# Two small weight loads issued by ScalarE in place of SyncE, at the head of a long-convolution and MLP kernel

## The chip, the cores and the metric

The kernel runs on one core of one Trainium2 chip. The metric is the device time of one execution in microseconds (us). The engines are named as in the profile: PE is TensorE (PEld its weight loads), ACT is ScalarE, DVE is VectorE, POOL is GpSimd and SP is SyncE. SP issues nearly all memory transfers; ACT can issue them as well, and in this kernel issues two. The data move on the core's 16 DMA engines. Rows marked SPq and ACTq show the time in which an engine issues a transfer, not the time in which the data move.

## The reference

Two layers stand in turn, each twice. Layer A is a gated long convolution: `k` is filtered with a four-tap causal filter per channel (`shift_k`), multiplied by `v`, convolved over the whole sequence with `ssm_k`, given a skip term `ssm_D`, and multiplied by the normalised input. Layer B is an MLP with a GELU.

```python
def _A_ref(q, k, v, shift_k, ssm_k, ssm_D):
    k_pad = jnp.pad(k, ((0, 0), (ks - 1, 0), (0, 0)))
    for t in range(ks):
        k_shift = k_shift + k_pad[:, t:t + S, :] * shift_k[:, ks - 1 - t]
    kv = k_shift * v
    ...
    y = irfft(rfft(kv) * rfft(ssm_k))[:S]
    y = y + kv * ssm_D
    return q * y
x = A_q
x = x + _A_ref(_layernorm(x), A_k, A_v, A_shift_k, A_ssm_k, A_ssm_D)
x = x + _B_ref(_layernorm(x), B_w1, B_b1, B_w2, B_b2)
x = x + _A_ref(...)
x = x + _B_ref(...)
```

Here S is 2048, D is 512, the MLP is 1376 wide, and all inputs are bf16. `shift_k` is 512 x 4: four kilobytes.

## The kernel before, in words

Since `kv` depends on `k` and `v` alone, the convolution is computed once and used by both A layers. The program has two parts. In the first, an order written out by hand (the string `ORDER`, L18 to L20) says which named piece stands next and on which engine: `lk1.S` is the piece `lk1` on SP, `kT1e.A` the evacuation of `kT1` on ACT, `P3` a PE piece that takes the third PSUM buffer. Each engine runs its pieces in that order. The second part (from L676) is the MLP, with PE bound by its matmuls.

What matters here is the head of the first part. Before the `ORDER` begins, the prologue issues two transfers from ACT, `Ft` (a table, L185) and four copies of `ssm_D` (L186), and lets POOL clear `kT` (L192) and spread `ssm_D` into `Dz` (L194). Then the pieces:

- `lSK` loads the weights of the last 128 channels as one row of 512 numbers (1 KB, the view `SKr`). `bSK` (L407) is a matmul that copies this row to all partitions, the first thing that PE does; ACT evacuates it (`bSKe`). POOL's filter of those channels uses it (`tap`, L435).
- `lsT` loads the weights of all 512 channels with a channel in each partition, as 128 x 4 runs of four numbers (8 bytes each). POOL casts it (`sF`, L361), and DVE builds twelve diagonal matrices from it (`dg`, L417), the weights of the filter on PE.
- `lk0` to `lk3` load `k` in four quarters of 512 KB; `lh1` and `lh113` load three rows before each partition's `k` (`kh`). `lx0` loads the first quarter of the input (512 KB, from `in_A_q_dram`), `lv0` and `lv1` load `v` (1 MB each), `lK00` to `lK11` load `ssm_k`.
- `kT1`, `kT3`, `kT0`, `kT2` (L423) transpose three channel groups of the four quarters of `k` on PE, in that order, each after its load. ACT evacuates the first three, DVE the last. `kv10`, `kv21`, `kv11`, `kv00` (L506) are the filter on PE, and DVE multiplies their results by `v` (L512).
- `s00` takes the layernorm sums of the first quarter of the input on ACT (L469 to L472). On ACT it stands behind the three evacuations and ahead of `U1S0e`, the evacuation of the convolution's first stage, for which PE waits.

Every transfer that SP or ACT issues has one of eight completion counters, named DMAHW0 to DMAHW7, which are handed out in turn in the order of the program text: `Ft` has 0, `ssm_D` 1, `lSK` 2, `lk1` 3, `lsT` 4, and so on. The ninth transfer has counter 0 again, and its issuer first waits until the transfer that had it before has landed.

Of the kernel before, what the change touches and what calls it, by code (L numbers as in the profile page):

```python
# [104 lines left out]
def kernel(ctx: ExitStack, tc: tile.TileContext, A_q, A_k, A_v, A_shift_k, A_ssm_k, A_ssm_D,  # L105
                 B_x, B_w1, B_b1, B_w2, B_b2, out):
    nc = tc.nc
    P = 128
    _, S, D = A_q.shape
    F = B_w1.shape[1]  # L110
    KS = A_shift_k.shape[1]
    NT = S // P
    CT = D // P
# [25 lines left out]
    def at(off, dims, p0=0, n=P):  # L139

        return apf(arena, p0 * ROW + off // 2, [[ROW, n]] + dims)
# [17 lines left out]
    CK = CT - 1  # L159
# [15 lines left out]
    B1 = const.tile([P, FT], F32, name="B1")  # L175
# [7 lines left out]
    nc.gpsimd.memset(IDt[:], 1.0)  # L183
    nc.gpsimd.affine_select(IDt[:], IDt[:], [[-1, P]], ALU.is_equal, 0.0, base=0, channel_multiplier=1)
    nc.scalar.dma_start(Ft[:], F_h.ap().bitcast(BF16))  # L185
    nc.scalar.dma_start(apf(arena, 40 * K, [[32 * ROW, 4], [1, D]]), apf(A_ssm_D, 0, [[0, 4], [1, D]]))  # L186
    nc.gpsimd.memset(b1T[:], 0.0)
    h = KS - 1
# [86 lines left out]
    with tc.tile_pool(name="ps", bufs=1, space=bass.MemoryType.PSUM) as ps:  # L275
# [3 lines left out]
        def load(name, dst, src, nbytes, deps=(), eng="S", rank=0):  # L279
            return plan.add(name, {eng: 400}, deps, lambda it: nc.sync.dma_start(dst, src), dma=("copy", nbytes), rank=rank)  # L280
# [5 lines left out]
        def mm_evac(name, ns, deps, mms, dims, dst, bf=False, take=(), free_mm=(), edeps=(), rank=0, src=None):  # L286
            src = src or (lambda v: v)
            n = int(np.prod(dims))
            cost = {"A": 85 + 0.82 * n, "D": 50 + (0.53 if bf else 1.06) * n}
            pe = plan.add(name, {"P": ns}, deps, lambda it: mms(view(pf[it["slot"]["ps"]], dims, BF16 if bf else None)),  # L290
                          take=["ps"] + list(take), free=free_mm, rank=rank)
            ev = plan.add(name + "e", cost, [pe] + list(edeps),
                          lambda it: evac(it["eng"], dst(), src(view(pf[pe["slot"]["ps"]], dims, BF16 if bf else None))),
                          free=[(pe, "ps")], rank=rank)
            return pe, ev
# [47 lines left out]
        kd4 = k_d.rearrange(TOK, p=P)  # L343
# [3 lines left out]
        for c in range(NK):  # L347
            n = 64 // NK
            lK.append([])
            for par in range(2):  # L350
# [3 lines left out]
                                      dma=("small", 2 ** 21 // (2 * NK))))  # L354
        lk = [load(f"lk{q}", kn[:, 4 * q:4 * q + 4, :], kd4[:, 4 * q:4 * q + 4, :], 2 ** 19) for q in range(4)]
        lv = [load(f"lv{o}", uv[:, 8 * o:8 * o + 8, :], vd[:, 8 * o:8 * o + 8, :], 2 ** 20) for o in range(2)]
        lS = [load("lsT", sT[:], A_shift_k.rearrange("(ct p) k -> p ct k", p=P), 2 ** 17),
              load("lSK", SKr, apf(A_shift_k, CK * P * KS, [[P * KS, 1], [1, P * KS]]), 2 ** 13)]
        lS += [load(f"lh{p0}", kh[p0:p0 + n, :, :], apf(k_d, (16 * p0 - h) * D + CK * P, [[16 * D, n], [D, h], [1, P]]), 2 ** 17)
               for p0, n in ((1, 112), (113, 15))]  # L360
        sf = plan.add("sF", {"G": 100}, lS[:1], lambda it: nc.gpsimd.tensor_copy(sF[:], sT[:]))  # L361
        lW = load("lW", Wt[:], W_h.ap().bitcast(BF16), 2 ** 20)
        lX = load("lX", Wx[:], X_h.ap().bitcast(BF16), 2 ** 20)
        lH = load("lH", GPt[:], GP_h.ap().bitcast(BF16), 2 ** 16)
# [36 lines left out]
        for j in range(4):  # L401
            r = slice(8 * j, 8 * j + 8)
            KX.append([load(f"s{w}{j}", KSW[a::2, r, :], ZK[1 - a::2, r, :], 1.15 * 2 ** 19, KW[4 * j:4 * j + 4] + (KWp if j == 3 else []))
                       for w, a in (("a", 0), ("b", 1))])


        _, bSK = mm_evac("bSK", 250, lS[1:2], lambda o: nc.tensor.matmul(o, one[:], SKr, start=True, stop=True), [P * KS],  # L407
                         lambda: SK[:])
# [40 lines left out]
        kgm = plan.add("kgm", {"D": 1150, "G": 4200}, kg[-1:] + lv, gmul)  # L449
# [8 lines left out]
        lx0 = load("lx0", lna0, xd[:, 0:GT, :], 2 ** 19)  # L458
        lx1 = load("lx1", x1, xd[:, GT:2 * GT, :], 2 ** 19)
# [33 lines left out]
        s10, _ = first(1, x1, lx1)  # L493
# [24 lines left out]
        lM = load("lM", Mt[:], M_h.ap().bitcast(BF16), 2 ** 21, kvp)  # L518
# [5 lines left out]
        lx = load("lx", x_t[:], q_d.rearrange(TOK, p=P), 2 ** 21, USp)  # L524
# [284 lines left out]
```

## Time and profile before

| | us |
|---|---|
| median of three runs | 253.29 (253.15 to 253.44) |
| profiled execution, its own time | 253.65 |
| its span, first to last instruction | 251.9 |
| PE busy | 236.9 (94%) |
| ACT busy | 146.5 (58%) |
| DVE busy | 169.7 (67%) |
| first transfer issued (SP and ACT) | 0.80 |
| first filter matmul on PE (L506) | 13.22 |

PE is nearly always busy, but the first 20 us are not its own: there it waits for loads and for ACT and DVE. A gain or a loss at the head moves everything behind it, as long as no wait behind it takes it up. In a row of the time line, the first number is the start, the second the length, and the bracket at the end says how long the engine was idle before it and what ended that.

### The profile page before, as it was taken

The page shows a single profiled execution, that of the slowest core. Times are in us where ns is not written, and L with a number is a line of the kernel's source. Part 1 is how long each engine was busy: PE and PEld are TensorE (multiplying, and loading weights), DVE is VectorE, ACT ScalarE, POOL GpSimd, SP SyncE. Part 2 cuts the span into 40 slices and gives each one's busy share as a digit, 9 for nine tenths or more (in the row PEclk, how much of TensorE's full clock was granted, in tenths as well). Part 3 has the DMA queues.
Part 4 walks back from the last instruction along what each step waited for, and adds up shares of the span by engine and source line. Part 5 has one row for each costly group of instructions (what it writes and reads, how often), then busy time and mean ns, then how long its engine had stood idle before and what let it go on. Part 6 is the DMA issues. An engine that isn't in the chain of part 4 may idle for free.

```text
span 251.9 us, 5135 instructions
## 1 busy us (share of the span) xinstructions
PE 236.9 (94%) x2104; PEld 146.1 (58%) x2104; DVE 169.7 (67%) x319; ACT 146.5 (58%) x212; POOL 54.6 (22%) x52
## 2 busy tenths in 40 slices
PE   2688999999999999999999999999999999999995
PEld 1588767899998738844444444444444444444443
DVE  0335889989999794987889899886866862022022
ACT  3598899999999798903803803803703712712810
POOL 3199999510000011011111101110110110000000
DMA  5999994698929993022040403107006006001001
GB/s 130 367 349 183 239 428 191 209 390 300 232 44 181 175 318 113 0 48 39 1 83 0 86 0 61 22 0 86 1 28 139 3 25 143 0 23 64 0 21 62
DMA packets 53040, 30.15 MB, mean 120 GB/s; under 512 B 46642, under 2 KB 50456, under 8 KB 51736
## 3 DMA queue, kind: packets, MB, share of 16 engines
q1 hardware_dynamic: 52864, 29.73, 45.0%
q8 instruction: 16, 0.26, 0.4%
q10 hardware_dynamic: 152, 0.09, 0.1%
q14 instruction: 8, 0.07, 0.1%
HBM read 16.71 MB, written 2.10 MB: 75 GB/s over the span
## 4 chain that ended last, share of the span: by engine, by line
PE 70%; DVE 9%; ACT 8%; DMA 8%; issue 4%; ACTq 0%; SPq 0%; DVEq 0%
PE po L720 30%; PE ph L686 29%; DVE arena L218 4%; DMA arena<-in_A_q_dram 3%; DMA arena<-in_B_w_dram 3%; DVE T L555 2%; PE p L506 2%; PE p L336 2%; ACT arena L216 2%; ACT ZT L216 2%; DVE ZT L218 2%; DMA arena<-in_A_ssm_D_dram 2%; ACT xb L216 2%; ACT arena L469 1%; PE p L382 1%
## 5 line engine op out<-in xcount | busy, mean ns | idle before, releaser
L688 ACT ACTIVATE arena<-ph,B 128x512 bf16<-128x512 f32 (+5 forms) x110 | 63.5, 609 | 81.9 <-PE ph L686 81.8
L686 PE MATMUL ph<-arena 128*128 128x512 bf16 (+4 forms) x440 | 78.5, 336 | 0.9 <-DMA arena<-in_B_w_dram 0.5
L720 PE MATMUL po<-arena 128*128 128x512 bf16 (+2 forms) x363 | 77.4, 372 | 0.0
L686 PEld LDWEIGHTS <-arena 128*128 128x128 bf16 (+1 forms) x440 | 40.5, 100 | 38.0 <-DMA arena<-in_B_w_dram 1.0
L720 PEld LDWEIGHTS <-arena 128*128 128x128 bf16 (+1 forms) x363 | 35.4, 98 | 40.5
L725 DVE TENSOR_TENSOR arena<-po,arena 128x512 bf16<-128x512 f32 (+1 forms) x33 | 21.5, 673 | 43.6 <-PE po L720 43.6
L216 ACT ACTIVATE arena<-p 128x1024 bf16<-128x1024 f32 (+6 forms) x40 | 38.8, 1040 | 7.9 <-PE p L423 4.5
L250 POOL TENSOR_TENSOR lrsm<-lrsm,mhalf 128x4 f32<-128x4 f32 (+2 forms) x10 | 8.9, 885 | 96.6 <-DVE lrsm L244 96.6
L216 ACT ACTIVATE ZT<-p 128x1024 bf16<-128x1024 f32 (+1 forms) x22 | 21.6, 1038 | 0.1
L238 DVE BATCH_NORM_STATS2 lstm<-arena 128x6 f32<-128x512 bf16 x32 | 19.9, 681 | 0.2
L218 DVE CAST arena<-p 128x1024 bf16<-128x1024 f32 x15 | 17.8, 1221 | 1.6 <-PE p L382 1.4
L555 DVE TENSOR_TENSOR T<-xb,arena 128x2048 bf16<-128x2048 bf16 (+1 forms) x17 | 18.8, 1163 | 0.0
L564 PE MATMUL p<-arena,T 128*128 128x128 bf16 x256 | 16.5, 219 | 1.1 <-DVE arena L218 0.4
L250 POOL TENSOR_TENSOR lrsg<-lrsg,mhalf 128x4 f32<-128x4 f32 x8 | 8.1, 1014 | 40.8 <-DVE lrsg L247 40.8
L437 POOL TENSOR_TENSOR T<-arena,SK 128x2048 bf16<-128x2048 bf16 (+3 forms) x4 | 15.0, 3751 | 5.1 <-DMA arena<-in_A_k_dram 5.0
L216 ACT ACTIVATE xb<-p 128x1024 bf16<-128x1024 f32 x15 | 15.9, 1132 | 0.1
L564 PEld LDWEIGHTS <-T 128*128 128x128 bf16 x256 | 14.9, 98 | 1.7 <-issue 1.4
L238 DVE BATCH_NORM_STATS2 lstg<-arena 128x6 f32<-128x512 bf16 x24 | 14.8, 680 | 0.0
L218 DVE COPY arena<-p 128x2048 bf16<-128x2048 bf16 (+3 forms) x10 | 10.4, 1049 | 5.9 <-issue 3.7
L255 DVE TENSOR_SCALAR arena<-arena,lmvg,lrsg 128x512 bf16<-128x512 bf16 x28 | 9.7, 408 | 6.7 <-POOL lrsg L250 6.7
L255 DVE TENSOR_SCALAR arena<-arena,lmvm,lrsm 128x512 bf16<-128x512 bf16 x32 | 11.2, 409 | 2.3 <-POOL lrsm L250 2.3
L506 PE MATMUL p<-DG,arena 128*128 128x128 bf16 x192 | 11.4, 219 | 1.3 <-ACT ZT L216 0.9
(78 smaller groups left out, 222.8 us busy)
## 6 DMA issues: line engine op xcount, KB each, us to landing
arena<-arena SPq DMA_DIRECT2D x8, 512.0 KB, 4.5
arena<-in_A_k_dram SPq DMA_DIRECT2D x4, 512.0 KB, 6.7
arena<-in_A_v_dram SPq DMA_DIRECT2D x2, 1024.0 KB, 10.8
arena<-in_A_ssm_k_dram SPq DMA_DIRECT2D x4, 512.0 KB, 7.1
arena<-tabM SPq DMA_DIRECT2D x1, 2048.0 KB, 12.5
arena<-in_A_q_dram SPq DMA_DIRECT2D x1, 2048.0 KB, 9.1
out_dram<-arena SPq DMA_DIRECT2D x15, 128.0 KB, 1.7
arena<-in_B_w_dram SPq DMA_DIRECT2D x1, 1376.0 KB, 7.8
```

The lines of the kernel that those rows point to most:

```text
L216: nc.scalar.activation(dst, src, AF.Copy)
L218: nc.vector.tensor_copy(dst, src)
L238: nc.vector.bn_stats(self.st[:, i, 0, :], x_t[:, GT * g + i, :] if src is None else src[:, i, :])
L250: nc.gpsimd.tensor_tensor(self.rs[:, a:b], self.rs[:, a:b], mhalf[:, a:b], ALU.pow)
L255: nc.vector.tensor_scalar(out=dst[:, i, :], in0=xs, scalar1=self.mv[:, i, 0:1], scalar2=self.rs[:, i:i + 1], op0=ALU.subtract, op1=ALU.mult)
L506: nc.tensor.matmul(o[:, i, :], w, DG[:, cc, t, :], start=t == 0, stop=t == KS - 1)
L555: eng.tensor_tensor(view(Tb[it["slot"]["T"]], [2, n, CW]), x2, kk, ALU.mult)
L564: nc.tensor.matmul(o[:, i, :], T[:, r, i, :], Mt[:, ka + i, 1 - r, :], start=r == 0, stop=r == 1)
L686: nc.tensor.matmul(o.rearrange("p (i t) -> p i t", t=P), W1t[:, ct, ft * P:ft * P + m], lt[:, a:b, ct, :], start=ct == 0, stop=ct == CT - 1)
L688: nc.scalar.activation(hT[0:m, ft, a * P:b * P], o, AF.Gelu_apprx_tanh, bias=B1[0:m, ft:ft + 1])
L720: nc.tensor.matmul(po[:, a:b], hT[0:m, ft, i * P:(i + 1) * P], W2t[0:m, ft, a:b], start=ft == 0, stop=ft == FT - 1)
L725: nc.vector.tensor_tensor(xs, po[:, a:b], xs, ALU.add)
```

## The change

`lSK` and `lsT` are no longer pieces on SP. The prologue issues them from ACT, `sT` first, between `Ft` and `ssm_D`; the two words are gone from `ORDER`, and everything else stands in the order of before. The two places in the list `lS` become `None`, which drops them from the plan's lists of dependencies (the waits themselves follow from the tiles that are read and written).

```diff
 ORDER = """
-lSK.S lk1.S lsT.S lk3.S lk0.S lk2.S bSK.P3 lh1.S bSKe.A lh113.S lx0.S kT1.P2
+lk1.S  lk3.S lk0.S lk2.S bSK.P3 lh1.S bSKe.A lh113.S lx0.S kT1.P2
...
     nc.scalar.dma_start(Ft[:], F_h.ap().bitcast(BF16))
+    nc.scalar.dma_start(sT[:], A_shift_k.rearrange("(ct p) k -> p ct k", p=P))
+    nc.scalar.dma_start(SKr, apf(A_shift_k, (CT - 1) * P * KS, [[P * KS, 1], [1, P * KS]]))
     nc.scalar.dma_start(apf(arena, 40 * K, [[32 * ROW, 4], [1, D]]), apf(A_ssm_D, 0, [[0, 4], [1, D]]))
...
-        lS = [load("lsT", sT[:], A_shift_k.rearrange("(ct p) k -> p ct k", p=P), 2 ** 17),
-              load("lSK", SKr, apf(A_shift_k, CK * P * KS, [[P * KS, 1], [1, P * KS]]), 2 ** 13)]
+        lS = [None, None]
```

On SP, the first transfers before (here `arena<-in_A_shift_k_dram` is `lSK`, `arena<-in_A_k_dram` a quarter of `k`, `arena<-in_A_q_dram` is `lx0`, `arena<-in_A_v_dram` is `lv0` and then `lv1`; a bracket names the counter that the issue waits for):

```order
L280 DMA arena<-in_A_shift_k_dram 1x512
L280 DMA arena<-in_A_k_dram 128x2048
L280 DMA sT<-in_A_shift_k_dram 128x4x4
L280 DMA arena<-in_A_k_dram 128x2048 x3
L280 DMA kh<-in_A_k_dram 112x3x128 [waits DMAHW0_49]
L280 DMA kh<-in_A_k_dram 15x3x128 [waits DMAHW1_49]
L280 DMA arena<-in_A_q_dram 128x2048 [waits DMAHW2_49]
L280 DMA arena<-in_A_v_dram 128x4096 [waits DMAHW3_49]
L280 DMA arena<-in_A_v_dram 128x4096 [waits DMAHW4_49]
```

And now:

```order
L282 DMA arena<-in_A_k_dram 128x2048 x4
L282 DMA kh<-in_A_k_dram 112x3x128 [waits DMAHW0_49]
L282 DMA kh<-in_A_k_dram 15x3x128 [waits DMAHW1_49]
L282 DMA arena<-in_A_q_dram 128x2048 [waits DMAHW2_49]
L282 DMA arena<-in_A_v_dram 128x4096 [waits DMAHW3_49]
L282 DMA arena<-in_A_v_dram 128x4096 [waits DMAHW4_49]
```

The four quarters of `k` now stand first on SP. The brackets read alike, but other transfers have the counters: in the text's order they are now `Ft` 0, `sT` 1, `SKr` 2, `ssm_D` 3, `lk1` 4. So `lh113` waits for `sT` where it waited for `ssm_D`, `lx0` still for the row of weights, `lv0` for `ssm_D` where it waited for `lk1`, and `lv1` for `lk1` where it waited for `sT`.

On ACT, the head of its program before:

```order
L185 DMA Ft<-tabF 128x320
L186 DMA arena<-in_A_ssm_D_dram 4x512
L191 ACT_TABLE_LOAD
L191 ACTIVATE act_73<-mhalf 128x1 [waits Pool_49]
L216 ACTIVATE SK<-p_122 128x512 [waits PE_49]
```

And now:

```order
L185 DMA Ft<-tabF 128x320
L186 DMA sT<-in_A_shift_k_dram 128x4x4
L187 DMA arena<-in_A_shift_k_dram 1x512
L188 DMA arena<-in_A_ssm_D_dram 4x512
L193 ACT_TABLE_LOAD
L193 ACTIVATE act_73<-mhalf 128x1 [waits Pool_49]
L218 ACTIVATE SK<-p_124 128x512 [waits PE_49]
```

The row of weights, which was the first transfer of SP's queue, is the third of ACT's, behind the table and the 512 runs of 8 bytes; `ssm_D` moved from second to fourth. PE still begins with the matmul that reads the row of weights, ahead of the transposes of `k`.

More of the change, by code (lines that the diff above doesn't have):

```diff
@@ new lines @@
+lk1.S  lk3.S lk0.S lk2.S bSK.P3 lh1.S bSKe.A lh113.S lx0.S kT1.P2 lv0.S sF.G lv1.S dg0.D dg2.D kT1e.A lK00.S kT3.P1 dg1.D lK01.S kT0.P0 kT3e.A kT2.P3 kT0e.A kg0.G kT2e.D s00.A kv10.P2 kv21.P1 kvm10.D kg1.G U1S0.P00 kv11.P3 U1S0e.A kvm21.D U1S1.P2 kvm11.D kv00.P0 U1S1e.A s01.G lK10.S kv01.P1 kvm00.D ka1.G s02.A U0S0.P31 kvm01.D U1S3.P2 lK11.S kv20.P0 U1S3e.D U0S0e.A kd0.P1 kd0e.A U0S3.P2 kvm20.D KS11.P3 U0S3e.A KS21.P1 kg2.G lX.S KS11e.D KS10.P0 KS21e.A KS00.P2 KS10e.A U2S0.P32 KS00e.D KS30.P1 U2S0e.A U2S3.P0 KS30e.D U0S2.P2 U2S3e.A KS20.P3 lH.S lW.S U2S1.P1 U0S2e.A KS20e.D lM.S KS31.P0 ka2.G lx1.S U2S1e.A kd4.P2 kd4e.A KS01.P3 KS50.P1 KS31e.A KS01e.D KS70.P2 KS70e.A KS41.P0 KS50e.D KS61.P3 KS41e.A KS40.P2 KS61e.D KS60.P1 KS40e.A KS51.P0 kg3.G KS60e.D KS71.P3 KS51e.A U1S2.P2 KS71e.A U2S2.P1 U1S2e.D U0S1.P0 U2S2e.A K211.P3 U0S1e.D K29.P2 K211e.A K210.P1 K29e.D K28.P0 K210e.A K214.P3 ka3.G K28e.A K24.P2 K214e.D K21.P1 K24e.A K215.P0 sa2.S K21e.D sb2.S K212.P3 K215e.A K20.P2 K212e.D lb0.S K23.P1 K20e.A lb1.S K22.P0 K23e.D K26.P3 K22e.A kgm.G K25.P2 s10.D K26e.A K27.P1 sb0.S sa0.S U2T0.P0 K27e.A K213.P3 K25e.A U2T1.P1 K213e.A sa1.S U1T0.P2 U2T0e.D B1.G sb1.S s11.G U2T1e.A sb3.S U3S0.P32 sa3.S U1T0e.D U1T1.P0 U3S0e.A X20.P10 U1T1e.D U3S2.P2 X20e.A X10.P31 U3S2e.D X21.P02 X10e.A U3S3.P1 T20.D0 X21e.A U3S1.P2 U0T0.P3 lx.S U3S1e.A T10.D1 X13.P00 U3S3e.A V20.P20 U0T0e.D X13e.A U3T0.S X23.P11 T21.D2 U0T1.P3 V20e.A T13.D0 X00.P02 X23e.A V10.P21 U0T1e.D X00e.A V21.P1 V10e.A T23.D1 X01.P00 V13.P3 V21e.A T00.D2 X02.P21 X01e.A V23.P1 X02e.D V13e.A X03.P02 T01.D0 V23e.A V00.P2 X03e.A T02.D1 X11.P30 V01.P1 V00e.A T03.D2 X12.P01 X11e.A V02.P2 V01e.D X12e.A U3T1.S X30.P32 T11.D0 V02e.A V03.P1 X30e.A T12.D1 X22.P00 V11.P2 V03e.A T30.D2 X31.P31 X22e.A Z01.S V12.P1 V11e.D X31e.A Z00.S T22.D0 X32.P02 V12e.A V30.P22 X32e.A T31.D1 Z10.S X33.P30 V22.P1 X33e.A T32.D2 Z03.S V31.P0 V22e.A T33b.D0 V32.P3 Z13.S V31e.A T33a.D1 V33b.P1 V30e.D V32e.A Z02.S V33a.P0 V33be.D V33ae.A TC0a.P2 TC0b.P3 Z12.S TC0ae.A TD0a.P1 TC1.P0 TC0be.D TD0ae.A Z11.S TD0b.P2 TC1e.D Y00.P3 TD0be.A TC3.P1 w3.S w1.S Y00e.A g00.D w2.S Y01.P2 TC3e.A w4.S TC2.P0 g01.D Y02.P3 h00.D Y01e.A Y10.P1 h01.D Y02e.A p00.G Y30.P2 TC2e.D Y10e.A p01.G Y12.P3 Y30e.A b00.D g02.D Y22.P1 Y12e.A LT0.P0 Y20.P2 b01.D Y22e.A LT0e.D h02.D Y32.P3 Y20e.A Y32e.D p02.G b02.D
```

1 line of the change is left out of this document (removed).

## The prediction

> **What bounds the kernel now.** I read the page first, for the whole.
>
> ```profile
> span 251.9 us, 5135 instructions
> PE 236.9 (94%) x2104; PEld 146.1 (58%) x2104; DVE 169.7 (67%) x319; ACT 146.5 (58%) x212; POOL 54.6 (22%) x52
> ...
> PE   2688999999999999999999999999999999999995
> ...
> DMA  5999994698929993022040403107006006001001
> ```
>
> PE is full from about 25 us on. The change touches the first three slices of 6.3 us each, where PE is not full and the DMA engines are. So the second view is the chain that ended last, from the start to 30 us (start, length, what).
>
> ```profile
> 1.18 4.02 DMA arena<-in_A_ssm_D_dram
> 5.22 0.34 SPq L280
> 5.61 7.80 DMA arena<-in_A_q_dram
> 13.43 0.73 ACT arena L469 x2
> 19.86 0.18 ACT arena L472
> 20.04 0.92 ACT ZT L216
> 21.00 3.73 PE p L506 x64
> ```
>
> The chain goes from `ssm_D` over its counter to the issue of `lh113` and `lx0`, through `lx0`'s landing at 13.41 to the sums of `s00` on ACT (13.43 to 20.04), and over `U1S0e` to PE's `kv00` at 21.00. Behind that it is computation, which a shift moves as a whole, down to the load of the MLP's weights and the MLP. So I carry what `s00`'s start gains or loses to the end one for one.
>
> The third view is the time line up to `s00`, in which two things stand close together.
>
> ```profile
> 0.80 0.35 SPq L280 DMA_DIRECT2D arena<-in_A_shift_k_dram  x1
> 0.80 0.35 ACTq L185 DMA_DIRECT2D Ft<-tabF  x1
> 1.18 1.21 ACTq L186 DMA_DIRECT2D arena<-in_A_ssm_D_dram  x1
> 1.21 0.38 SPq L280 DMA_DIRECT2D arena<-in_A_k_dram  x1
> 1.64 0.42 SPq L280 DMA_DIRECT2D sT<-in_A_shift_k_dram  x1
> 2.11 0.58 PE L407 MATMUL p<-arena,one 1*128 1x512 bf16 x1 [2.11 <-DMA arena<-in_A_shift_k_dram]
> 3.83 0.58 ACT L216 ACTIVATE SK<-p 128x512 bf16<-128x512 f32 x1
> 5.53 1.46 PE L423 MATMUL p<-IDt,arena 128*128 128x128 bf16 x12 [2.85 <-DMA arena<-in_A_k_dram]
> 7.03 1.45 ACT L216 ACTIVATE arena<-p 128x1536 bf16<-128x1536 bf16 x1 [2.62 <-PE p L423]
> 8.87 2.48 PEld L423 LDWEIGHTS <-arena 128*128 128x128 bf16 x24 [2.15 <-DMA arena<-in_A_k_dram]
> 10.37 2.79 ACT L216 ACTIVATE arena<-p 128x1536 bf16<-128x1536 bf16 x2 [1.90 <-PE p L423]
> 11.89 0.68 PEld L423 LDWEIGHTS <-arena 128*128 128x128 bf16 x12 [0.54 <-DMA arena<-in_A_k_dram]
> 13.43 0.63 ACT L469 ACTIVATE arena<-arena 128x512 bf16<-128x512 bf16 x1 [0.27 <-DMA arena<-in_A_q_dram]
> ```
>
> ACT's last evacuation of `k` ends at 13.16 and `s00` starts at 13.43: ACT waited only 0.27 us for `lx0`. So the start has two limits of nearly the same height, the landing of `lx0`, and the row PE `bSK`, `kT1`, ACT `kT1e`, `kT3e`, `kT0e`. Now the second limit hangs on the loads of `k` (5.53, 8.87), and the row of weights, there at 2.11, is early by 3.4 us.
>
> **The change, part by part.** SP loses two issues ahead of `k`. `lk1` goes out at 0.80 in place of 1.21, a gain of 0.41 us; `lk3` also passes the 0.42 us of `sT`. What the DMA engines carry stays the same in bytes, so I count 0.41 us for the landings of `k`, `lx0` and `v`, at most. It may be nothing, since `Ft` and `lk1` now begin together. It may also be more: `sT`'s 512 runs of 8 bytes stand between `lk1` and `lk3` on SP's queue, and there the DMA engines have holes (stretch, its length, PE clock, DMA share, GB/s at the end).
>
> ```profile
> 3.00:4.00 1.00, 0.00 (x0) 0.00 (x0) 0.00 (x0) 0.99 (x3) 0.00 (x0) 1.00 0.88 209
> 4.00:5.00 1.00, 0.00 (x0) 0.00 (x0) 0.00 (x0) 0.40 (x1) 0.00 (x0) 1.00 0.59 133
> 5.00:6.00 1.00, 0.47 (x5) 0.47 (x6) 0.00 (x0) 0.00 (x0) 0.71 (x3) 1.00 0.77 145
> 6.00:7.00 1.00, 0.99 (x10) 0.72 (x7) 0.00 (x0) 0.00 (x0) 0.85 (x4) 1.00 0.86 229
> ```
>
> From 4 to 7 us the missing share adds up to 0.41 + 0.23 + 0.14 = 0.78 us. If the data of `k` fill it all from another queue, the loads land 0.41 + 0.78 = 1.19 us earlier; I keep that as the end of the gain.
>
> ACT gains two issues of 0.35 and 0.42 us, or up to 1.21 us for one that is held up as `ssm_D`'s is. The table load behind them (1.28 us) has until `bSKe` can start, some microseconds, and nothing else waits for ACT so early; I cost them at nothing. If that cover is gone, `bSKe` and all ACT work behind it is later by what is left over.
>
> **The row of weights** is the term that decides. It is now third on ACT's queue. No row shows such a transfer there, so I bound its landing. From below: issued behind `Ft` and `sT`, at 1.18 + 0.42 = 1.60 us, and 1.31 us from issue to use as before (0.80 to 2.11), 2.91 us. From above: it waits until all four quarters of `k` are in, 11.89 - 0.41 = 11.48 us. The nearest row is the second transfer on ACT's queue, `ssm_D`: its 4 KB took 4.02 us, and landed at 5.20, just ahead of the 512 KB of `lk1` on SP's queue (used at 5.53), though the issue was over at 2.39. It did not slip through between the pieces of `lk1`, it came with its end. `sT` took as long, and `Ft`, the first on ACT's queue, much less (microseconds to landing at the end).
>
> ```profile
> sT<-in_A_shift_k_dram SPq DMA_DIRECT2D x1, 4.0 KB, 4.5
> Ft<-tabF ACTq DMA_DIRECT2D x1, 80.0 KB, 1.9
> ```
>
> So I read that the two queues take turns by a transfer's share on a DMA engine, not by its pieces. ACT's turns are `Ft`, `sT`, `SKr`, `ssm_D`; SP's are `lk1`, `lk3`, `lk0`, `lk2`. The third of ACT comes behind the third of SP if SP has the first turn, behind the second if ACT has it. A quarter of `k` takes (11.89 - 8.87) / 2 = 1.51 us where nothing else holds it up (an estimate: two loads between those rows). With `lk1` at 5.53 - 0.41 = 5.12 us, `lk3` ends at 6.63 and `lk0` at 8.14. Both first issues start at 0.80, and no row shows who will be first; I take SP, whose first transfer was in use at 2.11, when `Ft` (0.80 + 1.9 = 2.70) had not landed, though it is the smaller of the two. The row of weights lands at about 8.1.
>
> From there: `bSK` 0.04 + 0.58, `kT1` 1.46 (its quarter has long landed), `kT1e` 0.04 + 1.45, `kT3e` and `kT0e` 2.79, together 6.36 us. They run back to back on ACT, as `lk3` and `lk0` are in by then. `kT0e` ends at 8.14 + 6.36 = 14.50, and `s00`, at 13.43 before, starts 1.07 us later. `lx0` is there by then. The point of no change is a landing at 13.43 - 6.36 = 7.07 us.
>
> [...]
>
> **The other waits that moved.** `lh113` now waits for `sT`, `lx0` for the row of weights, `lv0` for `ssm_D`. All are SP's, and behind them stand `lv1` and `lK00`. `lx0` issues at about 8.2 in place of 5.61, and `lv0` when `ssm_D` lands, one turn later, 8.14 + 1.51 = 9.65 in place of 6.10. That is hidden as long as the DMA engines still have `k` to move, which they do until about 11.5; the time from the end of an issue to the first use of small data, 2.11 - 1.15 = 0.96 us, is less than the rest. If that cover goes, `lx0` and `v` land later by the hole. POOL needs `ssm_D`, then `sT`, and DVE the cast:
>
> ```profile
> 5.25 0.19 POOL L192 MEMSET arena<- 128x96 bf16 x1 [3.20 <-DMA arena<-in_A_ssm_D_dram]
> 6.84 0.20 POOL L361 CAST sF<-sT 128x16 f32<-128x16 bf16 x1
> 7.07 2.04 DVE L417 TENSOR_SCALAR DG<-IDt,sF 128x128 bf16<-128x128 bf16 x12 [7.07 <-POOL sF L361]
> 12.85 0.96 DVE L218 COPY arena<-p 128x1536 bf16<-128x1536 bf16 x1 [3.73 <-issue]
> 16.01 1.23 DVE L512 TENSOR_TENSOR arena<-p,arena 128x1024 bf16<-128x1024 f32 x1 [2.21 <-DMA arena<-in_A_v_dram]
> 18.67 2.36 DVE L512 TENSOR_TENSOR arena<-p,arena 128x1024 bf16<-128x1024 f32 x2 [1.43 <-DMA arena<-in_A_v_dram]
> ```
>
> From `ssm_D` (5.20) to the last diagonal (9.11) it is 3.91 us, so 9.65 + 3.91 = 13.56, before `kT0e` ends at 14.50, when the filter can start. The filter itself then starts 1.3 us later than at 13.22, but its results wait for `v` at 16.01 and 18.67 today, and that wait is as long or longer (2.21 and 1.43 us); it costs nothing beside `s00`.
>
> **The sum.** +1.07 us on a span of 251.9, 253.0; the execution around it lasts 1.75 us longer (253.65), and this execution stands 0.36 above the median. Against the median it is 253.29 + 1.07 = 254.4.
>
> **The rivals.** First, no change: ACT has the first turn. The row of weights lands with `lk3`, at 6.63, `kT0e` ends at 12.99, and `s00` starts with `lx0` at 13.43 - 0.41 = 13.02 at best: 252.9 to 253.3. For it speaks that `Ft` and SP's first issue both start at 0.80, so that the first turn is open; against it, that any further delay of 0.44 us brings the loss.
>
> Second, faster: the small pieces pass between those of `k`, and the row of weights lands under 6.0. Then the loads set the start, and by the holes above they gain between 0.41 and 1.19 us; I take 0.8, which is 252.5. For it speak the holes; against it, `ssm_D`'s 4.02 us. [...]
>
> Third, much slower: the turns go by single pieces, and `sT`'s 512 of them, 32 on each of 16 engines, alternate with the 32 rows of `k` there (4 x 128 / 16). Then `sT` ends with `k`, the row of weights lands at 9.7 or later, and `s00` starts 2.6 us late or more: 255.9 and up. The slow row of `ssm_D` would fit this too if its pieces were late in the queue, but it has so few that they should not take 4 us.
>
> **How the numbers follow.** The forecast (two or more loads of `k` ahead, a landing from 7.6 to 9.0) has 0.38, no change 0.28, faster 0.24, much slower 0.10. A measurement of this kernel can tell about 0.2% (0.5 us) from no change. So slower by over 0.2% has 0.48, within it 0.28, faster 0.24. The forecast's own range is 253.8 to 255.2. For 8 in 10 the range reaches down into the faster case, to 252.4, below which about a third of it lies (0.08), and up to 255.5, which leaves out the third rival (0.10): 252.4 to 255.5.
>
> **What would show it.** Right: PE's matmul of L407 starts at about 8.1 and waits for `in_A_shift_k_dram`; `kT1` follows it at once; ACT's three evacuations run without a gap; `s00` starts at about 14.5 with no wait for `in_A_q_dram`; PE's wait for ACT ahead of `kv00` grows by a microsecond. Wrong: L407 starts before 7.0 us; then the start follows `lx0`, and the DMA share from 4 to 7 us tells whether the loads gained. An L407 after 9.7, or holes in the DMA share around 11 us, is the third rival.

## The result, and the profile after

The changed kernel takes 262.31 us (median of 4 runs, 261.35 to 262.71), against 253.37 us (4 runs, 253.15 to 255.42) for the kernel before: a ratio of 1.0329, 95% interval 1.0268 to 1.0389. Here and below, a median counts every execution, while a ratio and its interval leave out those more than 1.5% above the fastest of the same kernel. The profiled execution took 262.13 us, with a span of 260.4 us, 8.5 us more than before.

The page of the changed kernel, its head, the granted clock of PE in 40 slices, and the one group of instructions that is new among the costly ones (its columns: busy time, mean ns of one | idle time before, and what ended it). Line numbers are one or two higher than before.

```profile
span 260.4 us, 5135 instructions
...
PEclk9975999999999999999999999999999999999999
...
L418 DVE TENSOR_SCALAR DG<-IDt,sF 128x128 bf16<-128x128 bf16 x12 | 9.9, 893 | 10.7 <-POOL sF L362 10.7
```

The instructions are the same in number. But the twelve diagonals, 2.04 us before, are busy for 9.9 us, and the granted clock, 1.00 all the way before, drops in the third and fourth slice (13 to 26 us). The time line of the changed kernel has the place:

```profile
7.38 0.58 PE L408 MATMUL p<-arena,one 1*128 1x512 bf16 x1 [7.38 <-DMA arena<-in_A_shift_k_dram]
8.43 0.19 POOL L194 MEMSET arena<- 128x96 bf16 x1 [6.38 <-DMA arena<-in_A_ssm_D_dram]
9.39 4.14 ACT L218 ACTIVATE arena<-p 128x1536 bf16<-128x1536 bf16 x3 [0.80 <-PE p L424]
10.47 0.20 POOL L362 CAST sF<-sT 128x16 f32<-128x16 bf16 x1 [0.51 <-DMA sT<-in_A_shift_k_dram]
10.70 9.85 DVE L418 TENSOR_SCALAR DG<-IDt,sF 128x128 bf16<-128x128 bf16 x12 [10.70 <-POOL sF L362]
10.73 7.92 POOL L438 TENSOR_TENSOR T<-arena,SK 128x2048 bf16<-128x2048 bf16 x2
15.30 0.63 ACT L470 ACTIVATE arena<-arena 128x512 bf16<-128x512 bf16 x1 [1.77 <-DMA arena<-in_A_q_dram]
20.12 6.68 PE L507 MATMUL p<-DG,arena 128*128 128x128 bf16 x64 [7.20 <-DVE DG L418]
```

Before, POOL's first two long multiplications (`kg0` and the first of `kg1`) and PE's filter stood like this:

```profile
12.02 7.95 POOL L437 TENSOR_TENSOR T<-arena,SK 128x2048 bf16<-128x2048 bf16 x2 [4.98 <-DMA arena<-in_A_k_dram]
13.22 3.75 PE L506 MATMUL p<-DG,arena 128*128 128x128 bf16 x64 [0.47 <-ACT arena L216]
```

There the diagonals were done at 9.11, and POOL began to multiply 2.9 us later, when the last quarter of `k` was in. Now `sT` lands at about 10.3 (issued at 1.22, 9.1 us to landing), `k` lands earlier (no wait for it stands ahead of POOL's 10.73), and DVE and POOL begin within 0.03 us of one another. The durations of single instructions (min/median/max in ns), first of the diagonals and of POOL's two multiplications in the changed kernel, then of the diagonals before:

```profile
L418 DVE TENSOR_SCALAR DG<-IDt,sF x12: 240/241/4183, 10.7 to 20.3; 128x128 bf16<-128x128 bf16 x12
```

```profile
L438 POOL TENSOR_TENSOR T<-arena,SK x2: 3876/3990/4105, 10.7 to 14.8; 128x2048 bf16<-128x2048 bf16 x1, 128x1920 bf16<-128x1920 bf16 x1
```

```profile
L417 DVE TENSOR_SCALAR DG<-IDt,sF x12: 247/247/254, 7.1 to 8.9; 128x128 bf16<-128x128 bf16 x12
```

Most of the twelve take 0.24 us as before (they overlap, so that twelve took 2.04 us). Two are held: the first takes 4.18 us, beside POOL's first multiplication (4.11 us), and the second 3.90 us, beside POOL's second (3.88 us). That is the excess of the group, 9.85 - 2.04 = 7.8 us. PE, which needs the diagonals, is idle for 7.20 us and starts the filter at 20.12 in place of 13.22. Then it is slow as well: 6.68 us for 64 matmuls that took 3.75. The stretches around that (from:to, length, PE, PEld, DVE, ACT, POOL busy, then PE clock, DMA share, GB/s):

```profile
10.00:11.00 1.00, 1.00 (x12) 1.00 (x11) 0.30 (x1) 1.00 (x2) 0.47 (x2) 1.00 0.03 5
...
15.00:16.00 1.00, 0.00 (x0) 0.00 (x0) 1.00 (x1) 0.70 (x2) 1.00 (x1) 0.96 0.97 410
16.00:17.00 1.00, 0.00 (x0) 0.00 (x0) 1.00 (x1) 0.94 (x4) 1.00 (x1) 0.50 0.98 410
25.00:26.00 1.00, 1.00 (x12) 1.00 (x10) 0.18 (x1) 0.00 (x0) 1.00 (x1) 0.50 1.25 197
27.00:28.00 1.00, 1.00 (x20) 0.99 (x18) 1.00 (x1) 0.72 (x1) 1.00 (x1) 1.00 0.29 44
```

The granted clock is 0.50 from 16 us, some 3 us into the gap, to 26 us, 6 us after PE has begun again. The chain that ended last, cut off at 34 us, runs over these two things alone:

```profile
19.09 0.99 DVE DG L418 x6
20.08 0.04 issue
20.12 6.68 PE p L507 x64
...
29.46 3.57 PE p L507 x64
```

The last row is `kv00`, at 21.00 before: 8.46 us later, nearly all of the span's 8.5. The filter starts 6.90 us later, its first 64 matmuls take 2.93 us longer, and 1.37 us come back, since PE now meets no wait ahead of `kv00` (0.87 us for ACT's `ZT` among them). From `kv00` to the end it is 230.9 us in both kernels.

### The profile page after: what moved, and what is told of

Its sections match the earlier page's. It is cut to its first block, busy times and chain, and to the rows that moved or that the text cites. A ratio compares the mean times of both kernels' runs of the same rounds, so it can differ in the third digit from the quotient of the medians.

```text
span 260.4 us, 5135 instructions
## 1 busy us (share of the span) xinstructions
PE 239.1 (92%) x2104; PEld 149.4 (57%) x2104; DVE 177.5 (68%) x319; ACT 146.6 (56%) x212; POOL 54.6 (21%) x52
## 4 chain that ended last, share of the span: by engine, by line
PE 71%; DVE 10%; ACT 5%; issue 3%; DMA 2%; SPq 1%; DVEq 0%; ACTq 0%
PE po L721 29%; PE ph L687 28%; PE p L507 5%; DVE arena L220 4%; DVE T L556 3%; DMA arena<-ZT 2%; ACT arena L218 2%; PE p L338 2%; ACT xb L218 1%; PE p L632 1%; ACT ZT L218 1%; DVE ZT L220 1%; PE p L565 1%; SPq L612 1%; PE p L383 1%
## 5 line engine op out<-in xcount | busy, mean ns | idle before, releaser
L507 PE MATMUL p<-DG,arena 128*128 128x128 bf16 x192 | 14.3, 244 | 7.2 <-DVE DG L418 7.2
L507 PEld LDWEIGHTS <-arena 128*128 128x128 bf16 x192 | 13.8, 111 | 7.5 <-issue 6.5
L418 DVE TENSOR_SCALAR DG<-IDt,sF 128x128 bf16<-128x128 bf16 x12 | 9.9, 893 | 10.7 <-POOL sF L362 10.7
```

The lines of the kernel that those rows point to most:

```text
L507: nc.tensor.matmul(o[:, i, :], w, DG[:, cc, t, :], start=t == 0, stop=t == KS - 1)
```

## The experiments

Two theories stood after the result. One: POOL's multiplications hold the diagonals, because both now run at one time. Two: the diagonals come late because of the load alone, and the rest is the row of weights and `lx0`, as the prediction had it.

**One move at a time.** Two kernels each make half of the change. The first issues the row of weights alone from ACT, behind `Ft`:

```diff
 # against the changed kernel
-lk1.S  lk3.S lk0.S lk2.S bSK.P3
+lk1.S lsT.S lk3.S lk0.S lk2.S bSK.P3
...
-    nc.scalar.dma_start(sT[:], A_shift_k.rearrange("(ct p) k -> p ct k", p=P))
...
-        lS = [None, None]
+        lS = [load("lsT", sT[:], A_shift_k.rearrange("(ct p) k -> p ct k", p=P), 2 ** 17), None]
```

> Only the row of weights (lSK) goes to ACT, behind Ft and ahead of ssm_D; sT stays on SP behind lk1. Theory A (the loss of the changed kernel comes from sT, whose 512 runs of 8 bytes land at 10.4 us on ACT's queue, so that POOL casts it late and starts its long multiplications at the very time at which DVE builds the diagonals, and DVE is held): here sT lands near 6 us as before, the twelve diagonals take about 2 us, PE has no long gap, and the time is 252.8 to 254.5. Theory B (the loss comes from the late row of weights, which holds PE and ACT): the row lands at 4 to 8 us here too, and the time is 256 or more.

254.67 us (10 runs, 252.25 to 260.01), ratio 1.0028 (0.9986 to 1.007): no change that can be told. The row is in at 4.28, and `s00` starts at 13.80, 0.37 us later than before. In its time line the diagonals are not held, but POOL begins only 0.27 us after they end (9.48 + 2.04 = 11.52):

```profile
9.48 2.04 DVE L417 TENSOR_SCALAR DG<-IDt,sF 128x128 bf16<-128x128 bf16 x12 [9.48 <-POOL sF L361]
11.79 7.96 POOL L437 TENSOR_TENSOR T<-arena,SK 128x2048 bf16<-128x2048 bf16 x2 [2.34 <-DMA arena<-in_A_k_dram]
```

With so small a margin, the one execution of 260.01 us may be the collision itself; it left no trace, so this is not shown.

The second issues `sT` alone from ACT; the row of weights stays first on SP:

```diff
 # against the changed kernel
-lk1.S  lk3.S lk0.S lk2.S bSK.P3
+lSK.S lk1.S lk3.S lk0.S lk2.S bSK.P3
...
-    nc.scalar.dma_start(SKr, apf(A_shift_k, (CT - 1) * P * KS, [[P * KS, 1], [1, P * KS]]))
...
-        lS = [None, None]
+        lS = [None, load("lSK", SKr, apf(A_shift_k, CK * P * KS, [[P * KS, 1], [1, P * KS]]), 2 ** 13)]
```

> Only sT goes to ACT, behind Ft and ahead of ssm_D; the row of weights stays first on SP. Theory A: sT lands at 9 to 10.5 us, the diagonals start at 10 to 10.8 and two of the twelve are held for about 4 us each by POOL's multiplications, PE's filter starts at 18 to 20 us, and the time is 259 to 263. Theory B: PE and ACT are early again, and the time is 253 to 255.

262.36 us (4 runs), ratio 1.0335 (1.0244 to 1.0426): the whole loss. Its time line:

```profile
2.11 0.58 PE L407 MATMUL p<-arena,one 1*128 1x512 bf16 x1 [2.11 <-DMA arena<-in_A_shift_k_dram]
8.19 0.19 POOL L193 MEMSET arena<- 128x96 bf16 x1 [6.15 <-DMA arena<-in_A_ssm_D_dram]
10.02 9.75 DVE L417 TENSOR_SCALAR DG<-IDt,sF 128x128 bf16<-128x128 bf16 x12 [10.02 <-POOL sF L361]
11.07 7.94 POOL L437 TENSOR_TENSOR T<-arena,SK 128x2048 bf16<-128x2048 bf16 x2 [1.09 <-ACT arena L217]
12.99 0.63 ACT L469 ACTIVATE arena<-arena 128x512 bf16<-128x512 bf16 x1 [0.62 <-DMA arena<-in_A_q_dram]
```

The row of weights is there at 2.11, `s00` starts at 12.99, earlier than the 13.43 of the kernel before, and still the loss is all there. So it does not lie with the row of weights, nor with `s00`. POOL begins at 11.07, when five of the twelve diagonals have not begun; two of these are held, one for 4.10 us (4097 ns), and the twelve take 9.75 - 2.04 = 7.71 us more than before. One thing came otherwise than expected: `sT` had landed at 6.8, not at 9 to 10.5. What made the cast late (9.79) was `ssm_D`, which landed at 8.16 and for which POOL waits ahead of its cast.

**The collision taken away.** The changed kernel, in which POOL first copies one number of the last diagonal, and so multiplies only after DVE has done them all:

```diff
 # against the changed kernel
+    gd = const.tile([P, 1], BF16, name="gd")
 ...
         def tap(t):
             m = kpart if t else ksum
+            if t == 0:
+                nc.gpsimd.tensor_copy(gd[:], DG[:, 1, 3, 0:1])
```

> The changed kernel, but POOL first copies one number of the last diagonal, so that its long multiplications start only when DVE has built all twelve. Theory A: the diagonals take about 2 us (10.7 to 12.8) in place of 9.85, PE's filter starts at about 13.8, the granted clock stays at 1.00, and what is left is lx0's landing (15.3 in place of 13.4 us): 254.5 to 256. Rival (the diagonals are slow for another reason, such as the transfers that land in the same memory): they still take about 10 us, POOL is later by as much, and the time is 262 or more.

255.8 us (4 runs, 254.33 to 257.23), ratio 1.0102 (1.0019 to 1.0186), and a span of 252.8:

```profile
10.24 2.04 DVE L419 TENSOR_SCALAR DG<-IDt,sF 128x128 bf16<-128x128 bf16 x12 [10.24 <-POOL sF L363]
12.55 7.94 POOL L441 TENSOR_TENSOR T<-arena,SK 128x2048 bf16<-128x2048 bf16 x2
13.38 3.75 PE L510 MATMUL p<-DG,arena 128*128 128x128 bf16 x64 [0.46 <-ACT arena L219]
14.39 0.63 ACT L473 ACTIVATE arena<-arena 128x512 bf16<-128x512 bf16 x1 [1.06 <-DMA arena<-in_A_q_dram]
```

The loads come nearly as late as in the changed kernel (the cast at 10.01 in place of 10.47), one wait of POOL is added, and the kernel is some 6 us faster. The diagonals are back at 2.04 us, the filter at 13.38, the clock at 1.00. What is left: `s00` waits for `lx0` and starts at 14.39, 0.96 us late, and the span is 0.9 us longer than before. That is near the 1.07 us which the prediction forecast in all, but by chance: there the row of weights was to cause it, and here `s00` waits 1.06 us for `lx0`.

**The collision alone.** The kernel before, with five extra multiplications of 128x512 on POOL right behind its cast, so that they lie beside the diagonals; all loads as before. Their results are overwritten by `kg0`:

```diff
 # against the kernel before
+        def beside():
+            nc.gpsimd.tensor_copy(sF[:], sT[:])
+            for i in range(5):
+                nc.gpsimd.tensor_tensor(view(Tb[0], [NT, P])[:, 4:8, :], kn[:, 4:8, CK * P:D],
+                                        apf(SK, 0, [[P * KS, P], [0, 4], [KS, P]]), ALU.mult)
-        sf = plan.add("sF", {"G": 100}, lS[:1], lambda it: nc.gpsimd.tensor_copy(sF[:], sT[:]))
+        sf = plan.add("sF", {"G": 100}, lS[:1], lambda it: beside())
```

> The kernel before, where the diagonals are built from 7.1 to 9.1 us beside an idle POOL, with five multiplications of 128x512 on POOL right behind its cast of sT (about 1 us each; their result is overwritten later). Theory A (a POOL multiplication holds the DVE instruction that builds a diagonal until it is over): the twelve take 4.5 to 6 us in place of 2.04, some single ones about 1 us in place of 0.25, and since DVE's next work starts at 12.85, the time changes by less than 1 us. Rival (the diagonals of the changed kernel are slow for another reason): they take about 2.0 us here.

261.7 us (4 runs), ratio 1.0346 (1.0271 to 1.0421) to 252.55 us: the loss of the change, made without the change. The expectation of under a microsecond was a miss. Its time line:

```profile
6.69 6.13 POOL L364 TENSOR_TENSOR T<-arena,SK 128x512 bf16<-128x512 bf16 x5
6.76 14.11 DVE L422 TENSOR_SCALAR DG<-IDt,sF 128x128 bf16<-128x128 bf16 x12 [6.76 <-POOL sF L362]
12.90 7.92 POOL L442 TENSOR_TENSOR T<-arena,SK 128x2048 bf16<-128x2048 bf16 x2
20.93 5.69 PE L511 MATMUL p<-DG,arena 128*128 128x128 bf16 x61 [3.55 <-DVE DG L422]
```

```profile
L422 DVE TENSOR_SCALAR DG<-IDt,sF x12: 241/1148/4102, 6.8 to 17.0; 128x128 bf16<-128x128 bf16 x12
```

I had counted on the diagonals to be done with the five instructions, 1.23 us each. But DVE got about two diagonals done in the time of one such: one that was held for about 1.15 us (the median of the twelve is 1148 ns), and one of 0.24 us that passed between two instructions of POOL. So ten were done when `kg0` began at 12.90, and the last two ran into it and `kg1`: they were held until 20.87, 7.97 us together, one of them 4.10. Two left over cost as much as five (`sT` alone) or all twelve (the changed kernel): what counted in these three runs was whether any were left when POOL's long instructions began, up to one for each of these.

**Another engine for the diagonals.** The changed kernel, in which ACT builds them, behind `kT0e`:

```diff
 # against the changed kernel
-... dg0.D dg2.D kT1e.A ... kT3.P1 dg1.D ... kT0e.A kg0.G
+... kT1e.A ... kT3.P1 ... kT0e.A dg0.A dg2.A dg1.A kg0.G
```

> The changed kernel, with the twelve diagonals built by ACT in place of DVE, behind its evacuation of kT0; all loads stay as changed. Theory (POOL's multiplication holds a DVE instruction of the diagonals' kind, and nothing else that runs beside it; ACT's three evacuations beside it took their usual 1.38 us each): the twelve ACT instructions take an ordinary time, about 0.25 us each, 3 us together, though POOL multiplies beside them the whole time. They start at 13.5, the filter begins at about 16.6, s00 at about 16.6 in place of 15.3; kv00 comes at about 24.2 (16.6 + 6.6 + 1.0), 3.2 us behind the kernel before, and the run takes 255.5 to 257.5. Rival (POOL's multiplication holds whoever builds the diagonals, since both read and write the same memory): single ACT instructions take about 4 us, the filter begins at 19 or later and the run takes 261 or more. A gap of PE from 12.9 to 16.6 us may lower the clock in either case, for at most 3 us more.

257.58 us (4 runs, 257.15 to 259.02), ratio 1.0186 (1.0132 to 1.0239), just above the 255.5 to 257.5 expected. Its time line, and the durations:

```profile
10.80 7.92 POOL L438 TENSOR_TENSOR T<-arena,SK 128x2048 bf16<-128x2048 bf16 x2 [0.64 <-ACT arena L218]
13.36 3.60 ACT L416 ACTIVATE DG<-IDt,sF 128x128 bf16<-128x128 bf16 x12
```

```profile
L416 ACT ACTIVATE DG<-IDt,sF x12: 392/395/412, 13.4 to 16.6; 128x128 bf16<-128x128 bf16 x12
```

POOL multiplies all the while (10.80 to 18.72), 4.11 us the first time, and no ACT instruction takes nearly as long: 392 to 412 ns (250 had been expected; without POOL beside them they were not measured). So it is not whoever writes these tiles that was held in the runs above, but DVE's instruction, for up to 4183 ns. It is no repair, as the diagonals now take 3.60 us of ACT ahead of `s00`.

**PE kept busy.** The changed kernel with 28 matmuls of 512 columns on PE in the gap, whose result nothing reads, to tell the wait from the clock:

```diff
 # against the changed kernel; in the ORDER: s00.A wm.P2 kv10.P2
+        def warm(it):
+            o = view(pf[it["slot"]["ps"]], [2, D])
+            for i in range(28):
+                nc.tensor.matmul(o[:, 0, :], IDt[:], kn[:, 8 + i % 4, :], start=True, stop=True)
+        plan.add("wm", {"P": 6000}, [], warm, take=["ps"])
```

> The changed kernel, but PE does 28 matmuls of 512 columns into the buffer that its filter is about to fill (the results are overwritten), while it would wait for the diagonals from 13.6 to 20.1 us. Theory A's last part (the clock of 0.50 from 16 to 26 us comes from PE's own gap and costs about 3 us): the clock stays at 1.00, the first 64 filter matmuls take about 3.7 us in place of 6.7, and the time is 258.5 to 260. Rival (the clock falls whatever PE does): the clock is 0.5 there as well and the time is 262 or more.

260.09 us (4 runs, 258.21 to 262.73), ratio 1.0247 (1.0153 to 1.0341). The row of the filter, and, from the same profile, two later stretches:

```profile
19.85 4.05 PE L512 MATMUL p<-DG,arena 128*128 128x128 bf16 x64 [1.17 <-ACT arena L473]
```

```profile
42.00:44.00 2.00, 2.00 (x47) 1.13 (x41) 1.76 (x2) 1.86 (x3) 2.00 (x1) 0.66 0.56 225
44.00:46.00 2.00, 2.00 (x44) 1.27 (x46) 1.23 (x1) 1.18 (x2) 1.92 (x2) 0.50 0.01 2
```

The filter still starts late, but keeps the full clock (1.00 from 14 to 26 us): 4.05 us for 64 matmuls in place of 6.68. `kv00` comes at 26.56, 2.90 us sooner than in the changed kernel. So the clock of 0.50 makes some 3 us of the loss, and the held diagonals the rest. In this execution the clock dropped later instead, between 42 and 50 us, and only 0.9 us of the gain was left in the span (259.5). Two others, whose mean granted clock was 1.00, took 258.2 and 258.9 us, where 258.5 to 260 was expected.

**Can the loads be put otherwise?** Four versions of the changed kernel try to bring the diagonals ahead of `kg0` again. First, `sT` as 128 pieces of 32 bytes in place of 512 of 8; the weights then stand in another order, and the filter computes with these:

```diff
-    nc.scalar.dma_start(sT[:], A_shift_k.rearrange("(ct p) k -> p ct k", p=P))
+    nc.scalar.dma_start(sT[:], A_shift_k.rearrange("(p ct) k -> p ct k", p=P))
```

> The changed kernel, but sT is loaded as one run of 32 bytes in each partition, 128 pieces in place of 512 with the same bytes (the channels then stand in another order, so the filter of the first 384 channels uses other weights: the computation is not the reference's). Theory C (the two queues take turns by single pieces, so that each of sT's 32 pieces on a DMA engine waits for a 4 KB row of k): 8 pieces wait for 8 rows, sT lands at 5 to 7 us in place of 10.4, the diagonals are done before POOL's multiplications begin, PE has no long gap, and the time is 252.5 to 255. Rival (turns by whole shares, as the prediction had it, or slow issue on ACT): sT lands at 9 us or later as before, and the time is 260 or more.

262.25 us (4 runs), ratio 1.0354 (1.0265 to 1.0443). A miss: `sT` lands at 8.2 in place of 10.3, later than the 5 to 7 expected, and it doesn't help, since POOL's cast comes at 9.74 all the same: it stands behind the clearing of `kT`, which waits for `ssm_D` (8.15), and the spreading of `Dz`. `lx0` does come sooner, and `s00` starts at 13.43 as before, which again changes nothing in the time.

Second, ACT's issues in the order `sT`, row, `Ft`, `ssm_D`:

```diff
-    nc.scalar.dma_start(Ft[:], F_h.ap().bitcast(BF16))
     nc.scalar.dma_start(sT[:], A_shift_k.rearrange("(ct p) k -> p ct k", p=P))
     nc.scalar.dma_start(SKr, apf(A_shift_k, (CT - 1) * P * KS, [[P * KS, 1], [1, P * KS]]))
+    nc.scalar.dma_start(Ft[:], F_h.ap().bitcast(BF16))
```

> The changed kernel with ACT issuing sT first, then the row of weights, then Ft and ssm_D. Theory C: sT still waits for some 32 rows of k, but without Ft's 8 pieces ahead of it, and lands at 7.5 to 9.5 us; the diagonals start by 10 us and are done before or soon after POOL's multiplications begin (10.7), so that at most one is held: 254 to 258. If the order on ACT's queue doesn't matter, sT lands at 10 us or later and the time is 260 or more.

262.48 us (4 runs), ratio 1.0358 (1.0287 to 1.043), where 254 to 258 was expected. `sT` lands at 5.9, sooner than expected, but `ssm_D` at about 9.2, and the cast comes at 10.88 behind it. Third, `ssm_D`, row, `sT`, `Ft`:

```diff
-    nc.scalar.dma_start(Ft[:], F_h.ap().bitcast(BF16))
-    nc.scalar.dma_start(sT[:], A_shift_k.rearrange("(ct p) k -> p ct k", p=P))
-    nc.scalar.dma_start(SKr, apf(A_shift_k, (CT - 1) * P * KS, [[P * KS, 1], [1, P * KS]]))
     nc.scalar.dma_start(apf(arena, 40 * K, [[32 * ROW, 4], [1, D]]), apf(A_ssm_D, 0, [[0, 4], [1, D]]))
+    nc.scalar.dma_start(SKr, apf(A_shift_k, (CT - 1) * P * KS, [[P * KS, 1], [1, P * KS]]))
+    nc.scalar.dma_start(sT[:], A_shift_k.rearrange("(ct p) k -> p ct k", p=P))
+    nc.scalar.dma_start(Ft[:], F_h.ap().bitcast(BF16))
```

> The changed kernel with ACT's four transfers in another order: ssm_D, the row of weights, sT, Ft. Theory A (all of the loss is the meeting of the diagonals on DVE with POOL's multiplications, and the time at which POOL can cast sT, set by the later of ssm_D and sT, decides it): ssm_D lands by 4 us and sT by 7, POOL casts by 7.5, the diagonals are done in 2 us before POOL's multiplications begin near 10.7, and PE has no long gap: 252 to 254, perhaps a little under the kernel before, as the loads of k begin 0.4 us earlier. Rival (four small transfers on ACT's queue cost the loss in any order, by way of lx0 or the row of weights): 256 or more.

261.3 us (6 runs), ratio 1.0311 (1.025 to 1.0372) to 254.15 us, where 252 to 254 was expected. `ssm_D` is there at 5.1, and now the other gate is the late one:

```profile
5.15 0.19 POOL L194 MEMSET arena<- 128x96 bf16 x1 [3.10 <-DMA arena<-in_A_ssm_D_dram]
10.72 0.20 POOL L362 CAST sF<-sT 128x16 f32<-128x16 bf16 x1 [4.05 <-DMA sT<-in_A_shift_k_dram]
10.95 9.80 DVE L418 TENSOR_SCALAR DG<-IDt,sF 128x128 bf16<-128x128 bf16 x12 [10.95 <-POOL sF L362]
```

Fourth, the order with `sT` first, and POOL's cast put ahead of the work that needs `ssm_D`, so that `sT` is the only gate:

```diff
 # besides the order of the second version
-    nc.gpsimd.memset(kT[:, :, :, 0:2], 0.0)
-    for cg in range(4):
-        nc.gpsimd.tensor_copy(apf(Dz, ...), apf(arena, ...))
+        def cast_first():
+            nc.gpsimd.tensor_copy(sF[:], sT[:])
+            nc.gpsimd.memset(kT[:, :, :, 0:2], 0.0)
+            for cg in range(4):
+                nc.gpsimd.tensor_copy(apf(Dz, ...), apf(arena, ...))
-        sf = plan.add("sF", {"G": 100}, lS[:1], lambda it: nc.gpsimd.tensor_copy(sF[:], sT[:]))
+        sf = plan.add("sF", {"G": 100}, lS[:1], lambda it: cast_first())
```

> The kernel of the run with sT first on ACT, but POOL casts sT ahead of the pieces that wait for ssm_D (the clearing of kT and the spreading into Dz stand behind the cast). Theory A, with ssm_D as the second gate: the cast comes at about 6 us in place of 10.9, the diagonals take about 2 us and end by 8.5, PE has no long gap; lx0 still waits for Ft (9.5 us), so 253 to 255.5. Rival (the diagonals were not held by POOL's multiplications but by what lands or runs at that time otherwise): no gain over 260.

254.59 us (10 runs, 253.14 to 257.05), ratio 1.0014 (0.9973 to 1.0056): no change that can be told from the kernel before, with both loads on ACT.

```profile
5.90 0.20 POOL L360 CAST sF<-sT 128x16 f32<-128x16 bf16 x1 [3.85 <-DMA sT<-in_A_shift_k_dram]
6.13 2.04 DVE L420 TENSOR_SCALAR DG<-IDt,sF 128x128 bf16<-128x128 bf16 x12 [6.13 <-POOL sF L360]
9.85 4.14 ACT L215 ACTIVATE arena<-p 128x1536 bf16<-128x1536 bf16 x3 [3.85 <-DMA arena<-in_A_ssm_D_dram]
11.44 7.94 POOL L440 TENSOR_TENSOR T<-arena,SK 128x2048 bf16<-128x2048 bf16 x2
14.04 6.43 PE L509 MATMUL p<-DG,arena 128*128 128x128 bf16 x64 [1.80 <-ACT arena L215]
```

The diagonals end at 8.17, 3.3 us ahead of POOL, as expected, and the large loss is gone. So the cast has two gates, `sT`'s load and, by POOL's order, `ssm_D`'s, and none of the orders run has both of them there in time. The filter begins at 14.04, as `kT1e` waits for `ssm_D`, and its first 64 matmuls are slow here too; in the profiled execution `kv00` comes at 23.14 in place of 21.00, and the span is 253.7, 1.8 us more than before. That execution, 255.37 us, is one of the slower of the ten; by the interval the loss is at most 1.4 us, and there may be none. No version beat the kernel before.

## Why the prediction was right or wrong

The sign was right, the size was not: 254.4 us, at most 255.5, was forecast, and it became 262.3. The sign was luck: the row of weights, from which it came, made `kT0e` 0.37 us late, and what made the loss of 8.5 us in the span stood in no term of the sum.

*The loads of `k`.* The gain was bounded at 0.41 to 1.19 us. In the version with 128 pieces POOL waits for the last quarter of `k` until 10.85, against 12.02 before: 1.17 us, the upper end; in the changed kernel POOL begins at 10.73 with no wait for `k` shown, so it was not much different there. It was not welcome: it brought `kg0` nearer to the diagonals.

*The row of weights.* Forecast at 8.1, with 7.07 as the point of no change; it came at 7.38. `kT0e` ended at 13.53, 0.37 us later than before. The landing was near the forecast, but whether by the turns from which it was read is not shown (see the last section), and the term on which the sum rested was worth a third of the 1.07 us given to it.

*`s00`.* Forecast 1.07 us later, "`lx0` is there by then". It was 1.87 us later, because of `lx0`: on SP, `lh113` stands ahead of it, and that one waits for `sT` (10.3), which no number of mine had followed. The row "hidden as long as the DMA engines still have `k` to move, which they do until about 11.5" failed with it: from 10 to 11 us the DMA engines were nearly idle (a share of 0.03).

*The other waits*, the step that failed. "From `ssm_D` (5.20) to the last diagonal (9.11) it is 3.91 us, so 9.65 + 3.91 = 13.56, before `kT0e` ends at 14.50". Two things in it were wrong. The last gate of the cast was `sT`, as well as `ssm_D`; that alone would have cost nothing, since the cast came at 10.47 against the 11.3 that follows from 13.56. And the 2.04 us of the diagonals were taken from a row in which POOL sat idle beside them. Beside POOL's multiplications they took 9.85. The row that would have told was not read: `kg0` at 12.02, the next work of POOL. By the prediction's own times the diagonals would have stood from 11.52 to 13.56, beside `kg0`. In the text `kg0` has the diagonals among its predecessors, but that sets an order and no wait, for POOL reads none of them. A margin of 2.9 us, not a semaphore, had kept them apart. With this step fell the path: the end was to follow `s00` one for one, but it followed the diagonals and PE's filter. In the version with `sT` alone on ACT, `s00` came 0.44 us sooner than before, and the loss was whole.

*PE's clock* was no term at all. A gap of 7.2 us on PE cost nearly 3 us more than its length (6.68 us for the 64 matmuls behind it, 3.75 before).

*The rivals.* The third came nearest: `sT`'s many pieces did land last, with a hole at 10 to 11 us, as it said. Its 255.9 and up covers the time, but for another reason, a row of weights that passes no earlier than 9.7, and that row was in at 7.4. No rival had two engines in each other's way.

What the trace shows of the hold is one instruction of DVE of 4183 ns, where the median diagonal takes 241, beside one multiplication of POOL of 4105 ns. In the changed kernel the diagonal is recorded as starting first, at 10.70, and POOL's multiplication at 10.73; in the version with `sT` first on ACT POOL's starts at 11.09 and the diagonal at 11.11. In both it was the diagonal that was held (4183 and 4131 ns). DVE's evacuation `kT2e` was not held: 0.96 us at 12.85 in the kernel before, beside `kg0`, and 0.94 us at 20.48 in the changed kernel, with no multiplication beside it. Why a diagonal waits for POOL, no run here shows. That POOL's multiplications hold the diagonals on DVE, the version with POOL behind the diagonals (2.04 us) and the one with POOL beside them (14.11 us) show; that ACT's are not held, the version with ACT does.

## What to carry to other kernels

When a load moves, ask of what it feeds not only whether it is still in time, but beside what it will then run: here a step of DVE that ended 4 us before PE needed it slid under two long instructions of POOL and became nearly five times as long (9.85 us in place of 2.04). An order in the program is not a wait: look for pairs that only a margin keeps apart, here one of 2.9 us, and write the margin down. And ask of a long gap on PE whether it costs more than its length: here one of 7.2 us cost nearly 3 us more.

## What the runs showed of the hardware

- In these runs a multiplication of POOL that met the diagonals held one of them for about as long as it lasted itself, be it 1.23 us (a median of 1148 ns for the twelve) or 4.11 us (4183 ns), while POOL was not slowed: 7.92 us for `kg0` and `kg1` beside the diagonals, 7.95 without.
- In the changed kernel the granted clock fell to 0.50 about 3.0 us into the gap of PE and came back 6.0 us after PE had begun again; in the versions with `sT` alone, with 128 pieces, with `sT` first and with `ssm_D` first it was 2.9 to 3.5 us and 3.4 to 5.3 us. In three executions profiled (`sT` alone, 128 pieces, PE kept busy) it fell at 42 to 44 us (for the first two once more) and was back by 51, although PE was busy in these stretches (with the extra matmuls 2.00 us of every 2 from 42 to 50, at a clock of 0.50 from 44 to 48); from `kv00` to the end it took 232.9 to 233.2 us there, against 230.2 to 231.4 in the others. Why PE lost its clock there is open.
- In the last version (`sT` first, cast first) the filter's first 64 matmuls took 6.43 us, about 100 ns each, as in the changed kernel at a granted clock of 0.50 (6.68 us), while the granted clock here reads 1.00 in every stretch, as from 15 to 17 us (21 matmuls):

```profile
15.00:17.00 2.00, 2.00 (x21) 2.00 (x20) 0.00 (x0) 1.94 (x6) 2.00 (x2) 1.00 1.03 430
```

  With the row alone on ACT the first 64 are slower than before too, 4.54 us: from 13 to 14 us PE does 9 matmuls in 0.81 us there, and 11 in 0.62 us in the version with POOL behind the diagonals, the clock at 1.00 in both. So in these two executions the clock's column does not show all of PE's pace; the count of matmuls does. Why is open as well.
- `sT`, 4 KB in 512 pieces, took from issue to landing 4.5 us third on SP's queue, 5.1 first on ACT's, 8.4 third, and second on ACT's 5.6 us with nothing but `ssm_D` behind it, but 8.2 to 9.1 us (four executions) with the row of weights behind it too. Neither turns by a transfer's share nor turns by single pieces give all of these, and the runs don't settle which rule does:

```profile
sT<-in_A_shift_k_dram ACTq DMA_DIRECT2D x1, 4.0 KB, 9.1
```
